# One operand of 16 blocks for the products of G and X in a chunked state recurrence

## The chip, the cores and the metric

The kernel runs on one core of one Trainium2 chip. The metric is the device time of one execution in microseconds, as the median of several executions; lower is better.

## The reference

The program is one attention-like recurrence followed by two feed-forward layers. Only the recurrence is touched by the change.

```python
B, H, S, D = 4, 8, 768, 40
for t in range(S):
    y[:, :, t] = einsum('bhd,bhde->bhe', r_t, state)
    Sa = einsum('bhde,bhe->bhd', state, a_t)
    state = state * w_t - einsum('bhd,bhe->bhde', Sa, b_t) + einsum('bhd,bhe->bhde', v_t, k_t)
x = y.transpose(0, 2, 1, 3).reshape(B * S, H * D)          # 3072 tokens of 320
x = moe(x)    # 8 experts of 1024, each token to its best one
x = moe2(x)   # 320 -> 2048 -> 320 with h * sigmoid(1.702 h)
```

## The kernel before

**Chunks.** The 768 steps are cut into 24 chunks of 32 steps. The 4 batches of 32 steps fill the 128 partitions, the 8 heads lie along the free axis. Inside a chunk the steps depend on one another through products of pairs of steps, so that a chunk needs four masked 32x32 matrices for each head and batch: G (k with a), X (v with r), Z (U with r) and the inverse T of a triangular matrix H (b with a). Every value is kept as a pair of fp16 numbers, high and low, and a product is the sum of three fp16 matmuls.

**From pair product to operand.** `pairs` makes the 32x32 products of one kind, 32 small matmuls for 8 heads, in the one PSUM bank "g". `masked` takes them out of the bank: a scalar_tensor_tensor on VectorE multiplies by the triangular mask into an fp32 tile `mx`, a copy to fp16 makes the high half, a subtraction the low half (`mgG`, `mgX`, `mgZ`). `bd` then spreads the four batches onto the diagonal of a 128x128 block for each head, by four operations, each a multiplication with a column of zeros and ones (`own`) that writes one stripe of 32 columns of all blocks. Each of the four may go to VectorE or ScalarE. The operands are `Gbd`, `Xbd`, `Zbd` and `Tbd`, [128, 2, 8, 128] fp16 each, one buffer each.

**Order of a chunk c.** `place(c)` spreads G and T (and fills `Nbd` and `KB`), `prep(c + 1)` loads k, v, r of the next chunk, splits and transposes them by DMA and makes the next G and X. `chain(c, g)` runs for two groups of four heads: W = Gbd v + (a with the state), then U by T, N and T again, then the state's update. `state` splits the new state for chunk c + 1. `output(c)` spreads X and Z and sums, in the PSUM bank "y", Xbd k + (r with the old state) + Zbd b; the sum is copied out to `Y` by VectorE. The state passes from chunk to chunk; the output doesn't feed the next chunk.

**What sets the order.** All instructions of the recurrence, the routing of tokens and the start of the first feed-forward layer go into a planner (`Plan`), which records reads and writes, and emits every engine's instructions in one fixed order. It works with a table of costs and with priorities by the longest path, and it chooses the engine wherever an operation is given as `either`. An engine then takes its instructions strictly in that order. Almost all rows of this stage show the line 234, where the planner issues. Names are therefore the key: `w<-vst,gbd` is the G product that opens a chunk's chain, `y<-kst,xbd` the X product of its output, `g<-rE,UE` its Z pairs, `y<-bst,zbd` (or `y<-xg,zbd`) its Z product, `S<-s,P` the new state. The copies of k stand in three buffers (`kst0` to `kst2`, chunk number modulo 3), those of v in two.

After the recurrence come the first feed-forward layer (lines 856 to 889) and the second (lines 1122 to 1165).

Of the kernel before, what the change touches and what calls it, by code (L numbers as in the profile page):

```python
# [9 lines left out]
F32 = mybir.dt.float32  # L10
# [456 lines left out]
F32 = mybir.dt.float32  # L467
F32R = mybir.dt.float32r
F16 = mybir.dt.float16
# [791 lines left out]
RING = 3  # L1261
PX, MX, MGX, SSB, V16B, UEB, SDB, PN = 4, 2, 2, 1, 2, 1, 2, 3
AHEAD = 1500
# [13 lines left out]
class Attn:  # L1277
# [7 lines left out]
    def __init__(self, tc, ctx, W, AB, KVR, keep, lent):  # L1285
# [6 lines left out]
        cp = self.cp = ctx.enter_context(tc.tile_pool(name="ac", bufs=1))  # L1292
# [13 lines left out]

        o64 = cp.tile([128, 64], F32, name="o64")
        nc.vector.memset(o64, 1.0)
        self.sel = cp.tile([128, 64], F32, name="sel")
        s2 = cp.tile([128, 64], F32, name="s2")  # L1310
        for dst, base in ((self.sel, 0), (s2, -32)):
# [44 lines left out]
        zero = lambda n, sh: self._zero(n, sh)  # L1356
        self.Gbd, self.Tbd, self.Nbd = (zero(n, [128, 2, 8, 128]) for n in ("gbd", "tbd", "nbd"))
        on = self.on
# [10 lines left out]
        for b2 in range(2):  # L1369
            for j in range(3):  # L1370
                r = slice(64 * b2, 64 * b2 + 64)
                nc.gpsimd.affine_select(self.pick[r, b2, j % 2, 40 * j:40 * j + 40], on[r, 0:40], pattern=[[1, 40]],
                                        compare_op=ALU.is_equal, fill=0.0, base=0, channel_multiplier=-1)
        self.Xbd, self.Zbd = (zero(n, [128, 2, 8, 128]) for n in ("xbd", "zbd"))

# [74 lines left out]
    def early(self, q):  # L1450
        nc = self.nc
        M = self.M[q // 2]
        u = slice(16 * (q % 2), 16 * (q % 2) + 16)
        BA = self.big()[:, 0:1280].rearrange("p (k h e) -> p k h e", k=2, e=40)
        nc.sync.dma_start(out=BA.rearrange("p k h e -> p k (h e)"), in_=self.AB[q])

        B, A = self.Bst[q % RING], self.Ast if q != 1 else self.Bst[RING - 1]
        for k, (st, f, lo, dup) in enumerate(((B, M["F"], 40, 80), (A, M["R"], 80, 40))):
            x = BA[:, k]
            nc.either(("vector", "tensor_tensor", (x, x, f[:, u, :]), dict(op=ALU.mult)))  # L1460
            self.twice(st, x, dup)
            nc.either(("vector", "tensor_tensor", (st[:, :, lo:lo + 40], x, st[:, :, 0:40]), dict(op=ALU.subtract)))
        bE = self.p1.tile([128, 16, 128], F16, tag="bE", name="bE") if q != 1 else \
            self.HU.bitcast(F16).rearrange("p t s -> p (t s)").rearrange("p (h x) -> p h x", h=16)
        aE = self.cp.tile([128, 16, 128], F16, name=f"aE{q}") if q < RING else self.E[q - RING]
        self.E[q] = aE
        nc.sync.dma_start_transpose(out=bE, in_=B.rearrange("p h x -> p (h x)"))
        nc.sync.dma_start_transpose(out=aE, in_=A.rearrange("p h x -> p (h x)"))
        H = self.pairs(bE, aE, 16)
        nc.scalar.activation(self.H[:, u, :], H, AF.Copy, scale=1.0 / (SK * SA))  # L1470
        N = self.pn.tile([128, 2, 16, 16], F16, tag="N")
        nc.scalar.activation(N[:, 0], H[:, :, 16:32], AF.Copy, scale=2.0 ** -6)
        nc.vector.scalar_tensor_tensor(N[:, 1], H[:, :, 16:32], 2.0 ** -6, N[:, 0], op0=ALU.mult, op1=ALU.subtract)
        self.N[q] = N

    def pairs(self, L, R, n):

        ps = self.pg.bank([n, 32], "g")
        for i in range(n):
            for b in range(4):  # L1480
                s = slice(32 * b, 32 * b + 32)
                self.nc.tensor.matmul(ps[s, i, :], lhsT=L[0:120, i, s], rhs=R[0:120, i, s], start=True, stop=True)
        return ps
# [67 lines left out]
    def masked(self, ps, scale, tag):  # L1551
        nc = self.nc
        n = ps.shape[1]
        x = self.p1.tile([128, n, 32], F32, tag="mx", name="mx", bufs=MX)
        nc.vector.scalar_tensor_tensor(x, ps, scale, self.mask.rearrange("p (o t) -> p o t", o=1).to_broadcast([128, n, 32]),
                                       op0=ALU.mult, op1=ALU.mult)
        g = self.p2.tile([128, 2, n, 32], F16, tag="mg" + tag, name="mg", bufs=MGX if tag == "X" else 2)
        nc.either(("scalar", "copy", (g[:, 0], x), {}), ("vector", "tensor_copy", (g[:, 0], x), {}))
# [3 lines left out]
    def prep(self, c):  # L1562
# [22 lines left out]
        C["rE"], C["k"], C["v"] = E[2], k, v  # L1585
        C["G"] = self.masked(self.pairs(E[0], aE, 8), 2.0 ** -6, "G")
        C["X"] = self.masked(self.pairs(E[1], E[2], 8), 2.0 ** -6, "X")

    def place(self, c):
# [3 lines left out]
        allh = slice(0, 8)  # L1593
        self.bd(self.Gbd, C["G"], allh)
        self.bd(self.Tbd, M["T"][c % 4], allh)
# [27 lines left out]
    def chain(self, c, g):  # L1623
# [6 lines left out]
        W = self.pw.bank([4, 64], f"w{g}")  # L1630
        self.mm3([(W[:, i, :], bd(self.Gbd, 4 * g + i), hl(C["v"], 4 * g + i)) for i in range(4)], True, c == 0)
        if c:
# [71 lines left out]
    def output(self, c, Sd, Y):  # L1704
# [5 lines left out]
        allh = slice(0, 8)  # L1710
        self.bd(self.Xbd, C["X"], allh)
        self.bd(self.Zbd, self.masked(self.pairs(C["UE"], C["rE"], 8), 2.0 ** -6, "Z"), allh)
        Yp = self.py.bank([8, 64], "y")
        self.mm3([(Yp[:, h, :], bd(self.Xbd, h), hl(C["k"], h)) for h in range(8)], True, False)
        if c:
# [210 lines left out]
```

## Time and profile before

| what | us |
|---|---|
| median of three runs (1107.86 to 1114.8) | 1113.67 |
| the profiled execution, its own time | 1103.53 |
| its span in the trace | 1101.8 |
| recurrence: from the start to the last copy of Y | 0 to 552 |
| end of the recurrence and start of the first layer | 552 to 600 |
| first layer | 600 to 760 |
| second layer | 760 to 1101.8 |

The profiled execution is a fourth run, a little faster than the three. The trace gives each instruction's start and end on its engine: PE is TensorE, DVE VectorE, ACT ScalarE. The four stretches follow each other, so that a microsecond taken out of the first moves everything behind it forward.

### The profile page before, as it was taken

How to read it: one execution, taken by the hardware profiler on the slowest of the kernel's cores; microseconds unless marked ns; L12 is line 12 of the kernel's file. 1: busy time of each engine (PE TensorE's matmuls, PEld its weight loads, DVE VectorE, ACT ScalarE, POOL GpSimd, SP SyncE). 2: the span in 40 equal slices, each digit the busy share in tenths (PEclk: the TensorE clock that was granted, in tenths of full speed). 3: DMA queues.
4: the chain of work that ended last, by engine and by line, in shares of the span. 5: the costliest groups of instructions: out<-in, count | busy, mean ns of one | idle time of the engine just before them, and what ended most of it. 6: DMA issues, size and time to landing. Idle time of an engine off the chain costs nothing. (4 is left out here: it accounts for less than half of the span.)

```text
span 1101.8 us, 37172 instructions
## 1 busy us (share of the span) xinstructions
PE 904.4 (82%) x15647; PEld 666.7 (61%) x15647; DVE 859.0 (78%) x2083; ACT 686.3 (62%) x1490; POOL 141.3 (13%) x225
## 2 busy tenths in 40 slices
PE   0167886876888887887569998998999999999995
PEld 0155665665667665666458877885555555555553
DVE  8998998999999999997565687777666666666652
ACT  4477998898899899886513364444443434343432
POOL 2000000020020030013031223212011111111101
PEclk9998897888666668788789999999999999999998
DMA  3669779689979789879525456445011111111100
GB/s 114 126 146 181 142 162 174 117 169 190 181 154 187 134 155 176 133 130 134 106 85 189 119 203 233 133 121 171 7 30 43 36 38 36 41 37 38 37 1 24
DMA packets 236014, 127.61 MB, mean 116 GB/s; under 512 B 219632, under 2 KB 222960, under 8 KB 234544
## 3 DMA queue, kind: packets, MB, share of 16 engines
q1 hardware_dynamic: 229680, 94.49, 46.5%
q0 software_dynamic: 6144, 30.54, 8.9%
q8 instruction: 125, 2.05, 0.8%
q14 instruction: 65, 0.53, 0.2%
HBM read 59.09 MB, written 12.16 MB: 65 GB/s over the span
## 5 line engine op out<-in xcount | busy, mean ns | idle before, releaser
L1138 ACT ACTIVATE sg<-t 128x512 f32<-128x512 f32 x96 | 60.5, 630 | 185.8 <-DVE t L1136 185.8
L1132 PE MATMUL h<-xT,WH 128*128 128x512 f16 x480 | 119.3, 379 | 3.0 <-DMA YS<-ys 2.3
L1156 PE MATMUL acc<-OH,gh 128*128 128x320 f16 x384 | 114.8, 299 | 0.5 <-ACT gh L1144 0.5
L1156 PE MATMUL acc<-OH,gl 128*128 128x320 f16 x384 | 114.8, 299 | 0.3 <-DVE gl L1148 0.3
L1156 PE MATMUL acc<-OL,gh 128*128 128x320 f16 x384 | 114.8, 299 | 0.0
L1136 DVE TENSOR_TENSOR t<-h,sB 128x512 f32<-128x512 f32 x96 | 66.2, 689 | 49.9 <-PE h L1132 49.9
L1156 PEld LDWEIGHTS <-gh 128*128 128x128 f16 x768 | 75.1, 98 | 43.6 <-ACT gh L1144 0.8
L1148 DVE TENSOR_TENSOR gl<-g,gh 128x512 f16<-128x512 f32 x96 | 66.3, 691 | 45.0 <-ACT gh L1144 45.0
L871 PE MATMUL h<-xT,split 128*128 128x128 f16 x1536 | 92.6, 221 | 5.4 <-DVE hl L874 2.3
L871 PEld LDWEIGHTS <-split 128*128 128x128 f16 x1536 | 89.7, 99 | 9.0 <-issue 4.1
L234 POOL DMA_INDIRECT XD<-XR,desti x24 | 31.2, 1302 | 468.5 <-ACT TT L234 206.9
L884 PE MATMUL y<-split,hh 128*128 128x320 f16 x384 | 82.3, 299 | 3.1 <-ACT split L846 1.3
L1132 PE MATMUL h<-xT,WL 128*128 128x512 f16 x288 | 77.8, 379 | 0.0
L1132 PEld LDWEIGHTS <-WH 128*128 128x128 f16 x480 | 46.5, 98 | 46.3 <-issue 2.6
L234 PE MATMUL w<-s,pick 128*128 128x160 f16 x368 | 62.8, 287 | 11.3 <-ACT s L234 4.1
L234 PEld LDWEIGHTS <-kb 64*128 64x128 f16 x2208 | 46.5, 101 | 33.0 <-issue 23.1
L234 PEld LDWEIGHTS <-tbd 128*128 128x128 f16 x1152 | 52.3, 106 | 21.9 <-issue 9.8
L1142 DVE SCALAR_TENSOR_TENSOR g<-h,sg 128x512 f32<-128x512 f32 x96 | 65.3, 680 | 0.0
L1144 ACT CAST gh<-g 128x512 f16<-128x512 f32 x96 | 59.2, 617 | 1.4 <-DVE g L1142 1.4
L1164 POOL DMA_INDIRECT out<-o,ti x24 | 23.4, 975 | 268.5 <-ACT o L1162 265.1
L884 PE MATMUL y<-split,hl 128*128 128x320 f16 x192 | 57.4, 299 | 0.0
L873 ACT ACTIVATE hh<-h 128x512 f16<-128x512 f32 x48 | 28.5, 594 | 38.8 <-PE h L871 38.5
(346 smaller groups left out, 2399.1 us busy)
## 6 DMA issues: line engine op xcount, KB each, us to landing
K<-in_KVR SPq DMA_DIRECT2D x24, 480.0 KB, 4.7
raw<-in_AB SPq DMA_DIRECT2D x13, 640.0 KB, 5.2
s<-in_wi SPq DMA_DIRECT2D x12, 512.0 KB, 4.6
s<-in_wo SPq DMA_DIRECT2D x10, 512.0 KB, 4.5
raw<-in_WU SPq DMA_DIRECT2D x6, 660.0 KB, 3.9
YS<-ys SPq DMA_DIRECT2D x24, 160.5 KB, 2.6
Sd<-s SPq DMA_TRANSPOSE x46, 4.4
raw<-in_KVR SPq DMA_DIRECT2D x1, 480.0 KB
```

Of the source, the lines that this page charges most:

```text
L234: r = self.made[i] = getattr(getattr(self.nc, e), op)(*a, **k)
L871: nc.tensor.matmul(h[:, f4, :], lhsT=a, rhs=b, start=(j == 0), stop=(j == 7))
L873: nc.scalar.activation(hh[:, s, :], h, AF.Relu)
L884: nc.tensor.matmul(y, lhsT=a[:, f, :], rhs=V(b, f), start=(n == 0), stop=(n == 23))
L1132: nc.tensor.matmul(h3, lhsT=a, rhs=r, start=(j == 0), stop=(j == 7))
L1136: nc.vector.tensor_tensor(t, hs[k], self.xs[steps[k][0]]["sB"], op=ALU.mult)
L1138: nc.scalar.activation(sgs[k], t, AF.Sigmoid, scale=1.702)
L1142: nc.vector.scalar_tensor_tensor(gs[k], hs.pop(k), 2.0 ** -4, sgs.pop(k), op0=ALU.mult, op1=ALU.mult)
L1144: nc.scalar.copy(ghs[k], gs[k])
L1148: nc.vector.tensor_tensor(gls[k], gs.pop(k), ghs[k], op=ALU.subtract)
L1156: nc.tensor.matmul(accs[c], lhsT=a[:, s], rhs=r[:, f, :], start=(f == 0 and j == 0), stop=(f == NF - 1 and j == 2))
L1164: sent.append(nc.gpsimd.indirect_dma_start(out=out, out_offset=bass.IndirectOffsetOnAxis(ap=X["ti"][:, c:c + 1], axis=0), in_=o, in_offset ...
```

## The change

G and X of a chunk are made together. `pairs` takes a list of operand pairs and writes 16 heads' worth of products into the whole bank "g". `masked` runs once over 512 columns instead of twice over 256, and `bd` spreads the 16 blocks into one operand `GXbd` [128, 2, 16, 128] with four operations of 1024 columns instead of eight of 512. That happens where G alone was spread before, in `place(c)`; `output(c)` reads blocks 8 to 15 of the same operand. The fp32 tile of `masked` now has a buffer for GX and one for Z (512 and 256 columns) in place of two that all three kinds shared (256 columns). A constant of the set-up borrows a piece of a large buffer. Z, T, N and KB are as before.

```diff
-PX, MX, MGX, SSB, V16B, UEB, SDB, PN = 4, 2, 2, 1, 2, 1, 2, 3
+PX, MX, MGX, SSB, V16B, UEB, SDB, PN = 4, 1, 2, 1, 2, 1, 2, 3
...
-        o64 = cp.tile([128, 64], F32, name="o64")
+        o64, s2 = self.bigs[0][:, 0:64], self.bigs[0][:, 64:128]
...
-        self.Gbd, self.Tbd, self.Nbd = (zero(n, [128, 2, 8, 128]) for n in ("gbd", "tbd", "nbd"))
+        self.GXbd = zero("gxbd", [128, 2, 16, 128])
+        self.Tbd, self.Nbd = (zero(n, [128, 2, 8, 128]) for n in ("tbd", "nbd"))
...
-    def pairs(self, L, R, n):
+    def pairs(self, what):
-        ps = self.pg.bank([n, 32], "g")
-        for i in range(n):
+        what = [(L[0:120, i], R[0:120, i]) for L, R, n in what for i in range(n)]
+        ps = self.pg.bank([len(what), 32], "g")
+        for i, (l, r) in enumerate(what):
             for b in range(4):
                 s = slice(32 * b, 32 * b + 32)
-                self.nc.tensor.matmul(ps[s, i, :], lhsT=L[0:120, i, s], rhs=R[0:120, i, s], start=True, stop=True)
+                self.nc.tensor.matmul(ps[s, i, :], lhsT=l[:, s], rhs=r[:, s], start=True, stop=True)
...
-        x = self.p1.tile([128, n, 32], F32, tag="mx", name="mx", bufs=MX)
+        x = self.p1.tile([128, n, 32], F32, tag="mx" + tag, name="mx", bufs=MX)
...
-        C["G"] = self.masked(self.pairs(E[0], aE, 8), 2.0 ** -6, "G")
-        C["X"] = self.masked(self.pairs(E[1], E[2], 8), 2.0 ** -6, "X")
+        C["GX"] = self.masked(self.pairs([(E[0], aE, 8), (E[1], E[2], 8)]), 2.0 ** -6, "G")
...
-        self.bd(self.Gbd, C["G"], allh)
+        self.bd(self.GXbd, C["GX"], slice(0, 16))
...
-        self.mm3([(W[:, i, :], bd(self.Gbd, 4 * g + i), hl(C["v"], 4 * g + i)) for i in range(4)], True, c == 0)
+        self.mm3([(W[:, i, :], bd(self.GXbd, 4 * g + i), hl(C["v"], 4 * g + i)) for i in range(4)], True, c == 0)
...
-        self.bd(self.Xbd, C["X"], allh)
-        self.bd(self.Zbd, self.masked(self.pairs(C["UE"], C["rE"], 8), 2.0 ** -6, "Z"), allh)
+        self.bd(self.Zbd, self.masked(self.pairs([(C["UE"], C["rE"], 8)]), 2.0 ** -6, "Z"), allh)
...
-        self.mm3([(Yp[:, h, :], bd(self.Xbd, h), hl(C["k"], h)) for h in range(8)], True, False)
+        self.mm3([(Yp[:, h, :], bd(self.GXbd, 8 + h), hl(C["k"], h)) for h in range(8)], True, False)
```

**What the planner makes of it.** The number of instructions on VectorE falls from 2713 rows to 2608, on ScalarE from 1691 to 1625; TensorE has the same 33233. Of the spreading operations of G and X, 86 were on VectorE and 106 on ScalarE; of the 96 of GX, 58 are on VectorE and 38 on ScalarE. Other work changes engine with it: VectorE gets 3 more spreading operations of T and Z together and 3 more splits of U, and gives 7 of `kb`, 2 other copies of k, v, r and the state, and 5 of the 1280-column copies of a and b to ScalarE. Of the copies to fp16 in `masked`, 23 of 72 were on VectorE, and now 18 of 48 (7 of them wide).

VectorE before, in the middle of the recurrence, where G of chunk 13 is spread (`mgG_1`). The copy `Y_0<-y` is that of chunk 10's output:

```order
L234 TENSOR_SCALAR s160_209<-S320_217 128x8x2x40
L234 SCALAR_TENSOR_TENSOR TT_3_248<-split1_152,TT_3_248 128x256
L234 TENSOR_TENSOR s160_209<-S320_217,s160_209 128x8x40
L234 SCALAR_TENSOR_TENSOR XR_0_278<-Y_0_275,sc_0_281,XR_0_278 128x256
L234 SCALAR_TENSOR_TENSOR XR_0_278<-Y_0_275,sc_0_281,XR_0_278 128x64
L234 TENSOR_SCALAR kb_226<-kst1_203,par_211 128x16x40
L234 TENSOR_TENSOR S321_218<-s_0_265,P_1_242 128x320
L234 TENSOR_SCALAR gbd_219<-mgG_1_258,own_212 128x16x32
L234 SCALAR_TENSOR_TENSOR Y_0_275<-y_0_234,split2_153 128x320
L234 TENSOR_SCALAR s161_210<-S321_218 128x8x2x40
L234 TENSOR_TENSOR K_0_249<-K_0_249,F_173 128x320
```

It stands behind the spreading of chunk 13's G. The same engine after the change, where GX of chunk 12 is spread (`mgG_0`; `Y_0<-y` is again chunk 10's output):

```order
L234 SCALAR_TENSOR_TENSOR mxG_0_250<-g_0_235,mask_214 128x512
L234 TENSOR_TENSOR s160_207<-S320_215,s160_207 128x8x40
L234 SCALAR_TENSOR_TENSOR XR_0_273<-Y_0_269,sc_0_276,XR_0_273 128x256
L234 TENSOR_REDUCE split1_152<-raw2_151 128x8x8
L234 SCALAR_TENSOR_TENSOR XR_0_273<-Y_0_269,sc_0_276,XR_0_273 128x64
L234 TENSOR_REDUCE split1_152<-raw1_150 128x8x8
L234 SCALAR_TENSOR_TENSOR Y_0_269<-y_0_231,split2_153 128x320
L234 TENSOR_TENSOR mgG_0_251<-mxG_0_250,mgG_0_251 128x512
L234 TENSOR_TENSOR S321_216<-s_0_259,P_1_239 128x320
L234 STREAM_TRANSPOSE split1_152<-split1_152 128x32x32
L234 TENSOR_SCALAR s161_208<-S321_216 128x8x2x40
L234 TENSOR_SCALAR gxbd_217<-mgG_0_251,own_210 128x32x32
```

The copy of the output moved from behind chunk 13's operand to ahead of chunk 12's.

TensorE before, at the start of chunk 13's chain (`w0<-vst1`); `y<-kst2,xbd` is the X product of chunk 11:

```order
L234 MATMUL y_0_234<-kst2_204,xbd_228 128x54
L234 LDWEIGHTS xbd_228
L234 MATMUL y_0_234<-kst2_204,xbd_228 128x54
L234 LDWEIGHTS gbd_219
L234 MATMUL w0_0_260<-vst1_206,gbd_219 128x54
```

The X product of chunk 11 stands among the first products of chunk 13. After the change, the end of the same X product (the rows behind it, `y<-Sd0,rE`, are the next part of the same output):

```order
L234 MATMUL y_0_231<-kst2_202,gxbd_217 128x54
L234 LDWEIGHTS gxbd_217
L234 MATMUL y_0_231<-kst2_202,gxbd_217 128x54
L234 LDWEIGHTS rE_2_278
L234 MATMUL y_0_231<-Sd0_0_266,rE_2_278 32x40
```

and, 188 rows on, the start of chunk 12's chain (`w0<-vst0`):

```order
L234 MATMUL s_0_259<-vst0_203,kb_224 128x54
L234 LDWEIGHTS kb_224
L234 MATMUL s_0_259<-vst0_203,kb_224 128x54
L234 LDWEIGHTS gxbd_217
L234 MATMUL w0_0_254<-vst0_203,gxbd_217 128x54
```

The X product of a chunk now ends ahead of the next chunk's W in all 23 places, by 90 to 460 rows; before, it ended 102 to 1056 rows behind it. A chunk has some 960 rows on this engine.

## Rows read from the trace of the kernel before

**Rows 1.** The page, busy tenths in 40 slices of the span.

```profile
DVE  8998998999999999997565687777666666666652
ACT  4477998898899899886513364444443434343432
```

**Rows 2.** Busy time of each engine in stretches of the recurrence.

```profile
core 0: us, PE busy (x) PEld busy (x) DVE busy (x) ACT busy (x) POOL busy (x), PEclk, DMA share, GB/s
75.00:500.00 425.00, 342.84 (x9977) 278.39 (x9976) 396.16 (x1102) 382.56 (x909) 28.12 (x32) 0.78 0.92 158
500.00:552.00 52.00, 31.84 (x938) 27.33 (x933) 34.70 (x138) 29.79 (x75) 9.82 (x18) 0.79 0.74 119
```

**Rows 3.** Groups by line and shape, 0 to 560 us: busy us, mean ns, idle before.

```profile
L234 DVE SCALAR_TENSOR_TENSOR mx<-g,mask 128x256 f32<-128x256 f32 x72 | 29.8, 415 | 10.2 <-PE g L234 9.7 <-PE w L234 0.3
L234 DVE TENSOR_TENSOR mgG<-mx,mgG 128x256 f16<-128x256 f32 x24 | 10.0, 415 | 0.0
L234 ACT CAST mgG<-mx 128x256 f16<-128x256 f32 x15 | 6.2, 410 | 6.2 <-DVE mx L234 6.2
L234 DVE TENSOR_SCALAR gbd<-mgG,own 128x512 f16<-128x512 f16 x55 | 17.7, 348 | 0.0
L234 DVE TENSOR_SCALAR nbd<-N,upper 128x256 f16<-128x256 f16 x96 | 23.9, 277 | 0.0
L234 ACT ACTIVATE gbd<-mgG,own 128x512 f16<-128x512 f16 x41 | 28.5, 724 | 3.4 <-DVE mgG L234 3.4
L234 ACT ACTIVATE xbd<-mgX,own 128x512 f16<-128x512 f16 x65 | 47.8, 748 | 0.3 <-PE y L234 0.3
L234 ACT ACTIVATE kb<-kst,par 128x640 f16<-128x640 f16 x32 | 26.5, 837 | 0.6 <-DVE kst L234 0.6
L234 PE MATMUL w<-vst,gbd 128*128 128x54 f16 x576 | 29.7, 205 | 11.5 <-ACT gbd L234 7.0 <-ACT Ss L234 3.1 <-ACT kst L234 1.3
```

**Rows 4.** The page's costliest groups: forms of twice the width, in the second layer.

```profile
L1142 DVE SCALAR_TENSOR_TENSOR g<-h,sg 128x512 f32<-128x512 f32 x96 | 65.3, 680 | 0.0
L1144 ACT CAST gh<-g 128x512 f16<-128x512 f32 x96 | 59.2, 617 | 1.4 <-DVE g L1142 1.4
L1148 DVE TENSOR_TENSOR gl<-g,gh 128x512 f16<-128x512 f32 x96 | 66.3, 691 | 45.0 <-ACT gh L1144 45.0
```

**Rows 5.** VectorE's timeline: start us, length us, then the instruction.

```profile
248.36 0.61 DVE L234 TENSOR_SCALAR gbd<-mgG,own 128x512 f16<-128x512 f16 x2
252.98 0.86 DVE L234 TENSOR_SCALAR nbd<-N,upper 128x256 f16<-128x256 f16 x4
...
305.42 0.42 DVE L234 SCALAR_TENSOR_TENSOR mx<-g,mask 128x256 f32<-128x256 f32 x1 [0.34 <-PE w L234]
305.76 0.48 DVE L234 TENSOR_SCALAR ust<-w 128x320 f16<-128x320 f32 x1
...
1000.05 0.69 DVE L1136 TENSOR_TENSOR t<-h,sB 128x512 f32<-128x512 f32 x1 [0.69 <-PE h L1132]
1000.65 0.68 DVE L1142 SCALAR_TENSOR_TENSOR g<-h,sg 128x512 f32<-128x512 f32 x1
```

**Rows 6.** ScalarE's timeline, the same columns.

```profile
209.65 1.94 ACT L234 ACTIVATE gbd<-mgG,own 128x512 f16<-128x512 f16 x3
259.18 1.58 ACT L234 ACTIVATE kb<-bst,par 128x640 f16<-128x640 f16 x2
```

**Rows 7.** Tiles gbd, xbd, Y: ns shortest/median/longest, first and last start us.

```profile
L234 PE MATMUL w<-vst,gbd x576: 185/199/253, 56.3 to 516.8; 128*128 128x54 f16 x192
L234 PE MATMUL y<-kst,xbd x576: 185/186/253, 87.7 to 541.4; 128*128 128x54 f16 x192
L234 DVE SCALAR_TENSOR_TENSOR Y<-y,R x12: 474/482/492, 173.8 to 551.8; 128x320 f32<-128x320 f32 x12
```

**Rows 8.** TensorE's timeline at chunk 9's output.

```profile
254.37 0.41 PE L234 MATMUL g<-rE,UE 120*32 120x32 f16 x32
259.48 0.74 PE L234 MATMUL y<-bst,zbd 128*128 128x54 f16 x23
```

More of the change, by code (lines that the diff above doesn't have):

```diff
@@ L1305, in __init__ @@
         self.clear(self.one.rearrange("p a b -> p (a b)"))
-        o64 = cp.tile([128, 64], F32, name="o64")
+        o64, s2 = self.bigs[0][:, 0:64], self.bigs[0][:, 64:128]
         nc.vector.memset(o64, 1.0)
         self.sel = cp.tile([128, 64], F32, name="sel")
-        s2 = cp.tile([128, 64], F32, name="s2")
         for dst, base in ((self.sel, 0), (s2, -32)):
@@ L1373, in __init__ @@
                                         compare_op=ALU.is_equal, fill=0.0, base=0, channel_multiplier=-1)
-        self.Xbd, self.Zbd = (zero(n, [128, 2, 8, 128]) for n in ("xbd", "zbd"))
+        self.Zbd = zero("zbd", [128, 2, 8, 128])
         self.viol = keep.tile([128, 12], F32, name="viol")
@@ L1468, in early @@
         nc.sync.dma_start_transpose(out=aE, in_=A.rearrange("p h x -> p (h x)"))
-        H = self.pairs(bE, aE, 16)
+        H = self.pairs([(bE, aE, 16)])
         nc.scalar.activation(self.H[:, u, :], H, AF.Copy, scale=1.0 / (SK * SA))
@@ L1553, in masked @@
         n = ps.shape[1]
-        x = self.p1.tile([128, n, 32], F32, tag="mx", name="mx", bufs=MX)
+        x = self.p1.tile([128, n, 32], F32, tag="mx" + tag, name="mx", bufs=MX)
         nc.vector.scalar_tensor_tensor(x, ps, scale, self.mask.rearrange("p (o t) -> p o t", o=1).to_broadcast([128, n, 32]),
                                        op0=ALU.mult, op1=ALU.mult)
-        g = self.p2.tile([128, 2, n, 32], F16, tag="mg" + tag, name="mg", bufs=MGX if tag == "X" else 2)
+        g = self.p2.tile([128, 2, n, 32], F16, tag="mg" + tag, name="mg", bufs=MGX)
         nc.either(("scalar", "copy", (g[:, 0], x), {}), ("vector", "tensor_copy", (g[:, 0], x), {}))
```

## The prediction

> **What bounds the kernel now.** The change touches only the recurrence, 0 to 552 us, so I first ask what is full there. The page's forty slices [rows 1] show VectorE at eight or nine tenths from the start to slice 20 and ScalarE close to it from slice 5 on; both fall off behind the recurrence. The table by stretches makes that a number [rows 2]: from 75 to 500 us VectorE is busy for 396.16 of 425 us (93%), ScalarE for 382.56 (90%), the DMA engines have a mean share of 0.92 and TensorE, at a granted clock of 0.78 of full speed, is busy for 81%. No single chain sets the pace here: chunks follow each other every 20.0 us (the W product's rows, tile gbd, first start 56.3, last 516.8, 23 chunks [rows 7]), and the idle time in front of all the W products is 11.5 us, of which 7.0 us waited for the operand gbd [rows 3]. So the pace is set by the instructions of VectorE and ScalarE, with VectorE the fuller by a little. In the last stretch, 500 to 552 us, VectorE is busy for only 34.70 of 52 us [rows 2]: that is the latency of the last outputs, the last copy of Y starting at 551.8, 35.0 us behind the last W product [rows 7].
>
> **How an operation is to be priced.** An instruction's duration isn't what it takes from its engine. Two spreads of 512 columns on VectorE last 0.61 us together [rows 5] while one lasts 0.348 [rows 3]: the second starts 0.26 us behind the first. Four of 256 columns last 0.86 us, one 0.277: 0.19 us each. So 256 columns more cost 0.066 us, and one of 1024 should hold VectorE for 0.26 + 2 x 0.066 = 0.39 us, against 2 x 0.26 = 0.52 for the pair that it replaces. On ScalarE three of 512 columns last 1.94 us [rows 6], one 0.724 [rows 3], so 0.61 each; two of 640 last 1.58 us, one 0.837, so 0.74. By the durations 128 columns add 0.113 us, by the spacing 0.13; one of 1024 thus holds ScalarE for 1.06 to 1.14 us, and I take 1.1, against 1.22 for the pair. The masked reading of the bank: the operation behind a 256-column one starts 0.34 us later [rows 5], one of 512 columns in the second layer holds the engine for 0.60 us (1000.05 to 1000.65 [rows 5]), so a pair of 0.66 to 0.68 becomes 0.60. The same holds for the subtraction, which has the same 0.415 us at 256 columns [rows 3] and 0.691 at 512 [rows 4].
>
> **The sum, part by part.** *Spreading, VectorE:* 86 operations x 0.26 = 22.4 us before, 58 x 0.39 = 22.6 after: +0.2 us, since the planner now gives VectorE 60% of them instead of 45%. *Spreading, ScalarE:* 106 x 0.61 = 64.7 us, after 38 x 1.1 = 41.8: -22.9 us. *Mask and subtraction, VectorE only:* 24 chunks x 2 x (0.66 - 0.60) = -2.9 us. *Copies to fp16:* ScalarE's 49 narrow ones (0.410 us long [rows 3], some 0.31 apart as an estimate from the 0.1 by which its other operations overlap) become 17 wide (0.617 [rows 4], so 0.51) and 13 narrow: 15.2 to 12.7, -2.5 us; VectorE's are about even. *Work that changes engine:* priced by width from the same rows, VectorE's 3 more T and Z spreads and 3 more U splits (+2.0), 7 fewer kb (-2.0), 2 fewer copies of 640 (-0.8) and 5 fewer of 1280 columns (-3.7) make -4.5 us; the mirror image puts about 9 us onto ScalarE. *Matmuls:* the same ones, 576 W and 576 X; no term. *Set-up:* the two zeroed operands become one of the same size, and the constants that move are below 1.5 us on either engine, beside a load that VectorE waits for; nothing. **VectorE: 0.2 - 2.9 - 4.5 = -7.2 us. ScalarE: -22.9 - 2.5 + 9 = -16.4 us.**
>
> If VectorE stays the fuller engine, the recurrence shortens by its 7.2 us: 1103.5 - 7.2 = 1096.3 us against the profiled execution. That execution lies 10 us below the median, so on the median's scale 1113.67 x 1096.3 / 1103.53 = 1106.4; I say 1106. The bounds of this term: by spacing with the planner's exchange left out, 2.7 us; by half of what both engines save together, 11.8 us.
>
> By whole durations, as if each instruction began only when the one ahead had ended, VectorE saves more: spreads 86 x 0.348 - 58 x 0.49 = 1.5, masks 24 x (0.83 - 0.68) = 3.6, subtractions 24 x (0.83 - 0.69) = 3.3, and some 5 of the exchange, 13.4 us in all, which gives 1090.1 and 1100 on the median's scale. The row of four spreads in 0.86 us, 0.25 us less than four times one [rows 3, 5], speaks against it. The Trainium skill, "VectorE: DVE Perf Modes", section "The DRAIN you can't avoid", says that the next operation doesn't start until the pipeline has emptied, and adds that one that is not held starts earlier; by the first half the sum would be this larger one, by this case's rows it is the smaller.
>
> **What the change adds: a wait.** With one buffer for both operands, chunk c + 1's GX can be written only when chunk c's X product has read its half. Before, the two had nothing to do with each other: the X product's rows (tile xbd) start 31.4 us behind the W product's in the first chunk and 24.6 us in the last [rows 7], which is more than a period, so X of chunk c came behind W of c + 1 everywhere. Now X of c must end, four writes must follow, and only then may W of c + 1 start. X of c in turn waits until Y of c - 1 has left the bank "y", and that for Z of c - 1. So the output, which nobody waited for, becomes part of a loop over two chunks: W, U, transposed U, Z, Y, X, GX, W. Behind a W that waits on TensorE stand the whole chain of its chunk and the state, and behind the waiting spreads on ScalarE and VectorE whatever the planner put there. Can the loop hold 2 x 20 us? From the Z pairs to the last Z product chunk 9 needed 5.85 us (254.37 to 259.48 + 0.74 [rows 8]); add Y (0.48 [rows 7]), 24 X products of some 0.03 us each (23 Z products took 0.74 [rows 8]), four writes on two engines (2 x 0.39 and 2 x 1.1 side by side, 2.2 us): 9.3 us and a few hand-overs from Z's pairs to the next W, out of a period of 20. There is room, unless Z's pairs come late. So I take the wait as 0 in the forecast; its upper bound is the four writes in full, some 2 us in each of 23 chunks, 46 us. Also, G's mask now waits for the last of three transposes (r) where it needed only k; the planner has placed that earlier, and the price is in the same bound.
>
> **The rivals.**
> *More comes back than VectorE's part.* ScalarE is lightened by 16 us and hands the chain's small copies over sooner, so that VectorE, which waits for some of them, loses part of its 29 idle us; and since outputs can't lag, fewer of them remain in the last 52 us, of which 17 are idle on VectorE [rows 2]. With half of both engines' saving (11.8) and 5 us of that tail, 16.8 us: 1086.7, on the median's scale 1097. For it: the planner balances the two engines. Against: static order, and DMA at 0.92. The reading by durations ends in the same region (1100).
> *The loop binds: slower.* The place is the spreading of GX, between X of c and W of c + 1, which the order shows 90 to 260 rows (2 to 5 us) apart in all but one chunk. The price is the part of the four writes and of the longer mask, copy and subtraction (0.75 us more in a row by [rows 3, 4]) that W waits for: 1 us in each of 23 chunks makes 23 - 7.2 = +16, so 1119 and 1130 on the median's scale; 2 us each, 1153. It decides once Y of c - 1 leaves its bank less than about 3 us before the state for chunk c + 1 is ready. For it: W already waited 7.0 us for gbd [rows 3].
> *Something else sets the pace.* The DMA share of 0.92 [rows 2] holds the transposes of k, v, r, U and the state, which don't change; if their rate is the limit, nothing moves: 1113.
>
> **How the numbers follow.** Forecast 0.43, more comes back 0.29, nothing moves 0.11, the loop binds 0.17. The four runs before spread by 1%, so about 1% is what a measurement can tell from no change. The forecast lies 0.7% below, so it counts as the same with some of its width beyond 1%: faster 0.32 (the second case and a little of the first), same 0.51, slower 0.17. For 8 in 10 the range goes down to the fast rival's 1097 less the width of a few us in which the runs scatter, 1091, and up over no change into the cheap end of the loop, 1126.
>
> **What would show it.** Right: the 256-column masks of G and X gone, 24 of 512 columns at about 0.68 us; spreads of 1024 columns at about 0.49 us on VectorE and 1.15 to 1.2 on ScalarE; VectorE still above 90% busy in the middle and ScalarE clearly lower, near 87%; the last copy of Y some 7 us earlier; idle time in front of W products not above the 11.5 us of now. Wrong: idle time before W that waits for gxbd, of the order of a microsecond for each chunk, and idle spells of both engines between Y and the spreading; or a period of 20 us unchanged although both engines have become emptier.

## The result, and the profile after

The changed kernel takes 1122.89 us (six runs, 1121.37 to 1125.53), the kernel before 1113.54 in the same measurement (six runs, 1104.0 to 1114.8): a ratio of 1.0108, 95% interval 1.0083 to 1.0133. The forecast was 0.7% faster; it is 1.1% slower. The profiled execution of the changed kernel took 1125.17 us. That of before (1103.53) lies just under the fastest of its six runs, so the 21.6 us between the two profiles are more than the 9.4 us between the medians, and I use the profiles for where time lies and the runs for how much it is.

The page of the changed kernel, busy tenths in 40 slices, beside [rows 1]:

```profile
DVE  8997898799799799697655688677766666666652
ACT  4467797798699699686722456445344435343432
```

Busy time by stretches, columns as in [rows 2]:

```profile
75.00:500.00 425.00, 326.82 (x9437) 265.88 (x9437) 373.96 (x973) 352.61 (x798) 18.54 (x32) 0.76 0.87 152
500.00:552.00 52.00, 36.83 (x1105) 30.96 (x1104) 37.07 (x135) 33.65 (x81) 8.86 (x16) 0.82 0.78 161
```

VectorE was to stay above 90% from 75 to 500 us. It is at 373.96 of 425, 88%: not a fuller engine with less to do, but an emptier one. The groups by shape, 0 to 580 us, that answer to [rows 3, 4]:

```profile
L234 ACT ACTIVATE gxbd<-mgG,own 128x1024 f16<-128x1024 f16 x38 | 42.7, 1152 | 3.8 <-DVE mgG L234 3.6
L234 PE MATMUL w<-vst,gxbd 128*128 128x54 f16 x576 | 29.5, 206 | 16.8 <-ACT gxbd L234 11.8 <-ACT Ss L234 3.2 <-DVE bst L234 1.0
L234 DVE TENSOR_SCALAR gxbd<-mgG,own 128x1024 f16<-128x1024 f16 x58 | 26.3, 479 | 0.3 <-PE y L234 0.3
L234 DVE SCALAR_TENSOR_TENSOR mxG<-g,mask 128x512 f32<-128x512 f32 x24 | 16.4, 685 | 2.0 <-PE g L234 1.8
L234 DVE TENSOR_TENSOR mgG<-mxG,mgG 128x512 f16<-128x512 f32 x24 | 16.4, 684 | 0.9 <-ACT mgG L234 0.9
L234 ACT CAST mgG<-mxG 128x512 f16<-128x512 f32 x17 | 10.5, 616 | 3.0 <-DVE mxG L234 2.9
```

The sizes are those that were priced: 0.479 and 1.152 us for a spread, 0.685 for a mask. The W product now waits 16.8 us, of them 11.8 for gxbd (11.5 and 7.0 in [rows 3]). Most of the 11.8 stands in front of the very first W product, before any loop has begun. TensorE's rows there, before and after:

```profile
56.33 1.26 PE L234 MATMUL w<-vst,gbd 128*128 128x54 f16 x24 [2.08 <-ACT gbd L234]
62.62 1.26 PE L234 MATMUL w<-vst,gxbd 128*128 128x54 f16 x24 [8.41 <-ACT gxbd L234]
```

In the other 23 chunks W waits 3.4 us for gxbd, where it waited 4.9 for gbd. So the loss isn't a wait of W for its operand. The tiles, with first and last start, beside [rows 7]:

```profile
L234 PE MATMUL w<-vst,gxbd x576: 185/208/253, 62.6 to 550.6; 128*128 128x54 f16 x192
L234 DVE SCALAR_TENSOR_TENSOR Y<-y,R x12: 479/483/492, 170.8 to 569.1; 128x320 f32<-128x320 f32 x12
```

W starts 6.3 us later in the first chunk and 33.8 us later in the last; the last output follows 18.5 us behind the last W instead of 35.0. Cut at these three times (first W, last W, last Y), the recurrence reads as follows; the third busy figure is VectorE, the fourth ScalarE. Before:

```profile
0.00:56.30 56.30, 4.32 (x220) 3.47 (x220) 50.81 (x124) 27.33 (x38) 5.84 (x34) 1.00 0.51 117
56.30:516.80 460.50, 368.72 (x10673) 299.37 (x10674) 430.62 (x1217) 407.64 (x973) 36.82 (x47) 0.79 0.92 158
516.80:551.80 35.00, 17.02 (x463) 14.87 (x460) 18.52 (x65) 17.21 (x43) 0.93 (x4) 0.76 0.52 107
```

After:

```profile
0.00:62.60 62.60, 4.19 (x220) 3.45 (x220) 57.24 (x129) 28.69 (x39) 5.89 (x34) 1.00 0.54 129
62.60:550.60 488.00, 372.71 (x10754) 304.58 (x10754) 421.36 (x1131) 393.76 (x896) 27.40 (x48) 0.77 0.86 153
550.60:569.10 18.50, 14.67 (x376) 12.47 (x369) 14.90 (x50) 13.97 (x39) 0.00 (x0) 0.91 0.09 17
```

The end of such a stage is VectorE's busy time plus its idle time, and that sum splits the loss. Busy: 50.81 + 430.62 + 18.52 = 499.95 before, 57.24 + 421.36 + 14.90 = 493.50 after, 6.45 less. Idle between the first and the last W: 460.5 - 430.62 = 29.9 before, 488.0 - 421.36 = 66.6 after, 36.7 more. Idle in the tail: 16.5 before, 3.6 after, 12.9 less. Idle ahead of the first W is the same (5.5 and 5.4). Together -6.45 + 36.7 - 12.9 - 0.1 = +17.3 us, which is by how much the last Y moved (551.8 to 569.1). A further 4.3 us of the two spans' 21.6 lie behind it. Of these, 2.8 are the start of the first layer, 23.7 instead of 20.9 us after the last Y: a scatter of routed rows on GpSimd, behind which the last rows wait, began 0.3 us ahead of the last Y before (551.53) and begins 2.4 us behind it now (571.47).

### The profile page after: what moved, and what is told of

Read it like the earlier page. It is cut to its first block, busy times and chain, and to the rows that moved or that the text cites. A ratio compares the mean times of both kernels' runs of the same rounds, so it can differ in the third digit from the quotient of the medians.

```text
span 1123.4 us, 37005 instructions
## 1 busy us (share of the span) xinstructions
PE 909.1 (81%) x15647; PEld 671.1 (60%) x15647; DVE 853.1 (76%) x1993; ACT 672.0 (60%) x1411; POOL 131.7 (12%) x224
## 5 line engine op out<-in xcount | busy, mean ns | idle before, releaser
L234 POOL DMA_INDIRECT XD<-XR,desti x24 | 24.1, 1006 | 517.8 <-ACT V L234 278.9
L234 PE MATMUL w<-s,pick 128*128 128x160 f16 x368 | 59.0, 273 | 15.0 <-ACT Ss L234 6.2
L234 PEld LDWEIGHTS <-gxbd 128*128 128x128 f16 x1152 | 47.9, 107 | 23.6 <-ACT gxbd L234 14.4
```

Source lines behind the costliest of these rows:

```text
L234: r = self.made[i] = getattr(getattr(self.nc, e), op)(*a, **k)
```

## The experiments

Three theories. **Theory 1:** the tie (W of chunk c + 1 behind X of chunk c, behind Y and Z of c - 1, behind the transposed U) costs some 1%. **Theory 2:** the wide mask and its wait for r stand in the way of W. **Theory 3:** the planner's new order is worse by chance. Measurements fell on different chips and times, in which the kernel before took about 1095 or about 1112 us; each kernel is compared with the runs of before that stand beside it. The parts of the change and the old U (below) were measured only where before takes about 1095 us.

**Parts of the change alone.** *Mask alone:* G and X share bank, mask and split, and are spread apart as before.

```diff
-        self.bd(self.GXbd, C["GX"], slice(0, 16))
+        self.bd(self.Gbd, C["GX"][:, :, 0:8], allh)
...
+        self.bd(self.Xbd, C["GX"][:, :, 8:16], allh)
```

> G and X share one bank, one mask, one split, as in the change; the spreads are the old ones, four of 512 columns into gbd with place and four into xbd with output. Theory 1 (the shared operand ties W of chunk c + 1 to X of chunk c, which costs 1.3 us in each chunk): without the shared operand the tie is gone, period back to 19.9 us, last Y 35 to 38 us behind the last W, time 1108 to 1114. Theory 2 (G's mask waits for the transposed r, and the wide mask and split lie in the path to W): the cost stays, period above 21 us, 1120 to 1128. Theory 3 (another order of the planner, good or bad by chance): anything from 1103 to 1125, with no tie between X and W.

Measured 1096.89 us, ratio 1.0026 (0.9986 to 1.0065). W starts at 63.7 us as late as after the change, but the loss isn't there. The wide mask and its wait for r (theory 2) carry no 1% here. That alone doesn't settle theory 2, because the whole change costs only 0.3% in measurements of this kind (below); the last pair of kernels does.

*Full width without the tie:* an operand of 24 blocks, in which X has two places in turn. To make room, `mgG` has one buffer instead of two and some tiles of the set-up lie in borrowed memory.

```diff
+        self.GXbd = zero("gxbd", [128, 2, 24, 128])
...
-self.pairs([(E[0], aE, 8), (E[1], E[2], 8)])
+self.pairs([(E[1], E[2], 8), (E[0], aE, 8)][::-1 if c % 2 else 1])
...
-        self.bd(self.GXbd, C["GX"], slice(0, 16))
+        self.bd(self.GXbd, C["GX"], slice(8 * (c % 2), 8 * (c % 2) + 16))
```

> The change with an operand of 24 blocks: G always in blocks 8 to 15, X in 0 to 7 in even chunks and in 16 to 23 in odd ones, so that every write is still one of 1024 columns, but X of chunk c need only be read before the writes of chunk c + 2. To make room mgG has one buffer instead of two, and some small tiles of the set-up lie in lent memory. Theory 1 (tie): the tie is one period looser, the outputs may lag again, period at or below 19.9 us, and the saving of the width comes out: 1100 to 1110, faster than before. Theory 2 (long operations and the wait for r ahead of W): nothing changes, 1120 to 1126. Theory 3 (order by chance): 1103 to 1125 without a pattern.

1094.87 us, ratio 1.0013 (0.9974 to 1.0051). Without the tie there is no slowdown, as theory 1 says, with the same reservation; but the kernel isn't faster either, against what theory 1 expected of it.

*Tie with wide spreads, narrow masks:*

```diff
+        GX = C["GX"] = self.p2.tile([128, 2, 16, 32], F16, tag="mgG", name="mg", bufs=MGX)
+        self.masked(self.pairs([(E[0], aE, 8)]), 2.0 ** -6, "G", GX[:, :, 0:8])
+        self.masked(self.pairs([(E[1], E[2], 8)]), 2.0 ** -6, "G", GX[:, :, 8:16])
```

> One operand of 16 blocks with four writes of 1024 columns, as in the change, but G and X are made, masked and split apart (two of 256 columns each), into the two halves of one tile. Theory 1 (tie): tied as the change is, minus the small saving of the wide masks (2.9 us of VectorE): 1121 to 1128, period about 21.3 us, last Y under 25 us behind the last W. Theory 2 in the part that blames the wide mask and split: 1110 to 1116; in the part that blames the wait for r: 1120 to 1126 as theory 1. Theory 3: no pattern.

1102.75 us, ratio 1.0089 (1.0056 to 1.0122).

*The tie alone,* with the masks of the last one and eight spreads of 512 columns:

```diff
-        self.bd(self.GXbd, C["GX"], slice(0, 16))
+        for a in range(2):
+            self.bd(self.GXbd[:, a:a + 1], C["GX"][:, a:a + 1], slice(0, 16))
```

> The tie alone: one operand of 16 blocks, but masks and splits of 256 columns as before, and eight spreads of 512 columns, each over all 16 heads of the high or of the low half. As many operations of the same width as before, only that all eight stand between X of chunk c and W of chunk c + 1. Theory 1 (tie): slower than the change by what its width saved, 1126 to 1140, period above 21.4 us, last Y close behind the last W. Theory 2 (wide operations): near before, 1111 to 1117. Theory 3: no pattern.

1105.3 us, ratio 1.0111 (1.0076 to 1.0146). These four shared one chip: the two without the tie are at before's time, the two with it 0.9 and 1.1% above. The expected 1126 and more was reckoned from a measurement in which before took 1113; the ratio is what counts.

**The changed kernel again, and what sets the pace of before.** 

> The changed kernel once more, beside the others of this call on one chip, with a profile. Theory 1 (the tie costs about 1%): ratio 1.007 to 1.013, and last Y 15 to 22 us behind the last W. Theory 3 (chance of one measurement): ratio near 1.002, as in the two kernels without the tie.

1100.14 us, ratio 1.0035 (1.0001 to 1.007); last Y 21.0 us behind the last W. The tail is what theory 1 expected, the ratio is less (1.007 to 1.013 expected). A third measurement:

> The changed kernel a third time, to settle the size: it was 1.0108 against before on one chip and 1.0035 on another. If the price hangs on the chip's DMA latency, between 1.002 and 1.012 again, with the higher ratio where before is slower; last W to last Y 15 to 22 us.

1098.36 us, ratio 1.0027 (0.9991 to 1.0062). Where before takes 1095 us the change costs 0.3%, not 1%. The kernel before, unchanged, with a second profile:

> The kernel before with a profile on the same chip as the others of this call, so that its windows can be set beside theirs. All theories: within 1% of the other runs of the kernel before; period of a chunk about 2% under 19.9 us if the chip is the faster one of the first experiments.

1114.56 us in one run, while the other runs beside it had a median of 1095.38: single executions of the kernel before scatter by over 1%.

*Less VectorE work:* the low halves of X and Z are made only in the first two chunks.

```diff
+        if lo:
             nc.either(("vector", "tensor_tensor", (g[:, 1], x, g[:, 0]), dict(op=ALU.subtract)))
...
-        C["X"] = self.masked(self.pairs(E[1], E[2], 8), 2.0 ** -6, "X")
+        C["X"] = self.masked(self.pairs(E[1], E[2], 8), 2.0 ** -6, "X", c < 2)
```

> The kernel before without the subtractions that make the low halves of X and Z, from chunk 2 on (the old low halves are used): 44 VectorE operations of 0.415 us fewer, which hold the engine for 0.33 us each, 14.5 us. None of them feeds the next state. If VectorE's occupancy sets the pace, as the sum of the prediction assumed: 14 us shorter, ratio about 0.987. If something else does (DMA, or the chain from state to state): within 0.4% of before. A saving of 7 us of VectorE would then be worth nothing either.

1097.79 us, ratio 1.0035 (0.9996 to 1.0074): no gain from more VectorE work than the change saves. Its stretch from first to last W:

```profile
57.10:526.20 469.10, 366.78 (x10669) 298.14 (x10669) 421.25 (x1200) 400.12 (x951) 34.90 (x47) 0.80 0.93 160
```

Busy 9.4 us less than before's 430.62, idle 47.9 where it was 29.9: in this stretch, what is taken from the engine comes back as waiting. The tail is shorter, 18.3 us instead of 35.0, so that the last Y stands at 544.5 us against 551.8; but these two profiles come from different measurements, and by the runs nothing is gained.

*Fewer DMA transposes:* the state's transposes for the output stop after chunk 1.

```diff
+        if c < 2:
             nc.sync.dma_start_transpose(out=Sd.rearrange("p a h x -> p (a h) x"), in_=S16.rearrange("p a h x -> p (a h x)"))
```

> The kernel before without the transposes of the state for the output (Sd), from chunk 2 on (the old ones are used, so later outputs and with them the routing and the layers behind are other ones; what counts is the recurrence in the profile): 44 of some 200 DMA transposes fewer. If the DMA engines (0.92 busy) set the pace: the period falls by more than 1.5 us and the DMA share falls below 0.85 only a little, last Y 30 us or more earlier. If VectorE sets it: the period stays at before's, and only the DMA share falls.

1084.78 us, ratio 0.9912 (0.9881 to 0.9943), DMA share 0.75. The stretch between the W products is 453.5 us instead of 460.5, 0.3 us a chunk: less than the 1.5 that a DMA limit would have given, more than nothing. The later outputs are other ones and with them the routing, so the stretch counts here and not the ratio.

*A shorter chain:* the correction V no longer enters U.

```diff
-        times(Up, self.Tbd, V16, False, skip_group_check=True)
```

> The kernel before, with the last T product left out of the chain (T times V, the correction, so U is another one): V is still computed, masked and copied, but U and the state no longer wait for it. 24 matmuls a chunk fewer, the same instructions on VectorE and ScalarE. What counts is the recurrence in the profile. If the chain from state to state sets the pace: X to V to U takes 2.5 to 3 us of each group in the trace of before, so the period falls by 1.5 us or more, 35 us in all, ratio about 0.97. If an engine's occupancy (VectorE, ScalarE, DMA) sets it: period within 0.4 us of before's.

1099.75 us, ratio 1.0045 (1.0016 to 1.0075); W to W 458.9 us, at a mean granted clock of TensorE of 0.75 instead of 0.79, which may have taken back a part. The 1.5 us a chunk that a limit by the chain from state to state would have given aren't there. None of the three, taken alone, sets the pace.

**What the tie waits for.** Z from the transposed U of the chunk before, in two buffers, once in the changed kernel, once in the kernel before (the output is another one in both):

```diff
-self.pairs([(C["UE"], C["rE"], 8)])
+self.pairs([(self.C[max(c - 1, 0)]["UE"], C["rE"], 8)])
```

> The changed kernel, but Z is made from the transposed U of the chunk before (UE in two buffers; the output is another one, the number of instructions is the same). The tie between X of c and W of c + 1 stays, but what X waits for (Y of c - 1, hence Z of c - 1) no longer waits for a DMA transpose that was just issued. If the tie costs what it does because the transpose of U now lies in the loop of the state: the recurrence is back at or below before's, waits for UE near 0, ratio 0.995 to 1.002. If the tie costs by itself (engine order, long writes ahead of W): as the changed kernel, 1.004 to 1.011.

1086.13 us, ratio 0.9887 (0.9804 to 0.997, from four runs): faster than expected.

> The control to the run with the tie: the kernel before with Z made from the transposed U of the chunk before. There the transpose of U lies outside the loop, the output only lags: within 0.4% of before by every theory, unless the stream of DMA waits itself slows the state's chain, then up to 0.5% faster.

1096.49 us, ratio 0.9984 (0.9949 to 1.002). The two ran on one chip, beside the third measurement of the changed kernel (1.0027). With the tie and all of the width, but without the wait for U's transpose, the kernel is 1.1% faster than before, while the same edit gives the untied kernel 0.2%. The stretches first W to last W, last W to last Y, with the tie:

```profile
60.40:524.30 463.90, 378.59 (x10878) 309.35 (x10879) 431.33 (x1163) 395.23 (x913) 30.87 (x48) 0.78 0.92 161
524.30:527.70 3.40, 2.90 (x118) 2.45 (x114) 3.40 (x13) 3.40 (x11) 1.52 (x1) 1.00 0.00 0
```

and without:

```profile
61.80:538.60 476.80, 374.45 (x10922) 305.63 (x10923) 436.68 (x1259) 419.68 (x996) 37.76 (x48) 0.80 0.90 157
538.60:542.10 3.50, 3.50 (x96) 3.22 (x94) 2.74 (x9) 2.83 (x9) 1.61 (x3) 0.54 0.02 5
```

In both the tail is gone: the last Z needs no fresh U. With the tie VectorE's idle time between the W products is 32.6 us, without it 40.1: here the tie costs nothing.

**Other orders of the same work.** One number of the planner is changed, in the kernel before and in the changed one.

```diff
-HOLD = 0.2
+HOLD = 0.22
```

> The kernel before, with one number of the planner changed (it holds an engine for a more urgent operation up to 0.22 instead of 0.20 of an operation's cost): the same instructions in another order. If a plan's chance is worth 1% (theory 3): ratio anywhere between 0.99 and 1.01. If the planner's orders are about equally good and the differences come from the change's tie: 0.997 to 1.003.

1109.2 us, ratio 0.9972 (0.9941 to 1.0003).

> The changed kernel with the first of the two planner numbers changed (0.22). Theory 1 (tie with the transposed U in it): the price stays under another order, 1.003 to 1.011, waits for UE above 10 us, last Y 15 to 25 us behind the last W. Theory 3 (chance of one plan): ratio as scattered as for the kernel before and not on one side of it.

1129.17 us, ratio 1.0132 (1.0077 to 1.0188).

```diff
-BIAS = 0.7
+BIAS = 0.72
```

> As the run before, with the other number of the planner changed (the cost by which it compares two engines weighted 0.72 instead of 0.70): again the same work in another order, some operations on another engine. Theory 3: between 0.99 and 1.01. Else 0.997 to 1.003.

1107.64 us, ratio 0.9946 (0.9917 to 0.9974).

> The changed kernel with the second of the two planner numbers changed (0.72). Theory 1: 1.003 to 1.011 again. Theory 3: on either side of the kernel before, between 0.99 and 1.01.

1127.8 us, ratio 1.0122 (1.0062 to 1.0181). A plan's chance is worth up to 0.5% (the 0.4% of the kernels with less VectorE work and with the shorter chain lie within it), but the pairs don't overlap: three orders of the changed kernel lie 1.0 to 1.3% above, where before takes some 1112 us, two of them a little above what theory 1 expected. Theory 3 falls.

**The tie's price on one chip,** both kernels of full width:

> The untied kernel of full width (X in blocks 0 to 7 or 16 to 23 in turn) again, now on the same chip as the changed kernel, so that the two differ only in the tie (and in one buffer of mgG). Theory 1 (the tie with the transposed U in it is the price): ratio 0.995 to 1.003, and 0.3 to 1.2% below the changed kernel of the same call. Theory 3: no order between the two. That the width itself is worth nothing shows again if this one does not fall under 0.995.

1110.33 us, ratio 1.0003 (0.9978 to 1.0029).

> The changed kernel beside the untied one on the same chip. Theory 1: above it by 0.3 to 1.2%, by more where the kernel before takes 1112 us than where it takes 1095; ratio to before 1.003 to 1.012. Theory 3: within the interval of the untied one.

1124.07 us, ratio 1.0101 (1.0044 to 1.0158). In this measurement the tie costs 13.7 us, and without it the width is worth nothing. The untied kernel has the wide mask and the wait for r as well, so theory 2 falls. First to last W, last W to last Y, the untied kernel:

```profile
58.00:536.20 478.20, 368.73 (x10720) 302.46 (x10721) 423.36 (x1123) 393.01 (x906) 34.53 (x48) 0.80 0.88 158
536.20:553.30 17.10, 13.94 (x402) 11.36 (x399) 14.99 (x48) 14.38 (x39) 0.00 (x0) 1.00 0.24 51
```

and the changed one beside it:

```profile
62.60:547.60 485.00, 373.32 (x10754) 304.10 (x10754) 421.43 (x1131) 394.15 (x896) 27.87 (x48) 0.77 0.86 154
547.60:565.80 18.20, 14.41 (x377) 12.20 (x369) 14.89 (x50) 14.03 (x39) 0.00 (x0) 0.91 0.09 17
```

VectorE idles 54.8 us between the W products without the tie and 63.6 with it.

## Why the prediction was wrong, point by point

**The prices of the operations were right.** VectorE's busy time fell by 6.45 us (forecast 7.2), ScalarE's from 27.33 + 407.64 + 17.21 = 452.18 to 28.69 + 393.76 + 13.97 = 436.42, 15.8 us (forecast 16.4). The reading by whole durations would have had 13.4 us for VectorE. The changed kernel's own rows show the spacing too: four spreads of 1024 columns in 1.67 us, 0.479 for one, so 0.40 apart (0.39 priced).

```profile
262.63 1.67 DVE L234 TENSOR_SCALAR gxbd<-mgG,own 128x1024 f16<-128x1024 f16 x4
```

The Trainium skill, "VectorE: DVE Perf Modes", section "The DRAIN you can't avoid", says that the next operation starts only behind the emptied pipeline, and adds that one that is not held starts earlier. These rows go with the second half: a spread starts 0.40 us behind the last, which takes 0.479.

**The first step that failed: "If VectorE stays the fuller engine, the recurrence shortens by its 7.2 us".** VectorE at 93% was read as the pace. The untied kernel of full width has the saving and no shorter time (1.0013, 1.0003): between the W products VectorE idles 462.6 - 423.31 = 39.3 us in its first profile and 54.8 in its second, against 29.9 and 464.2 - 429.89 = 34.3 in the two of before. Taking 9.4 us of that stretch's work from VectorE in the kernel before gave 1.0035, with 18 us more idle time. These stretches leave out the tail; that nothing was gained is by the runs. VectorE's remaining 7% were waits for other engines and for DMAs, and taking work from VectorE brought no gain. Fewer DMA transposes, less VectorE work and a shorter state chain each moved the stretch between the W products by -7.0, +8.6 and -1.6 us, where a plan's chance is about 5 us. Which of them would have to shrink together stays open.

**The second, which made the sign: "I take the wait as 0 in the forecast".** The loop was seen and priced by its length (9.3 us out of a period of 20), as if only a loop longer than the period could cost. Where before takes some 1112 us, as in the measurement that the forecast was made for, the tie costs 13.7 us at full width (1.0003 against 1.0101 on one chip). Where before takes some 1095 us, the tie by itself costs 1.1% (1.0111), but at full width its price isn't clear of noise (1.0027 and 1.0035 with it, 1.0013 without). VectorE's idle time between the W products is much the same there: 35.6 and 42.0 us with the tie (third and second measurement), 39.3 without (*Full width without the tie*). The three in this order:

```profile
62.50:518.40 455.90, 360.91 (x10754) 295.76 (x10754) 420.33 (x1131) 393.53 (x896) 29.60 (x47) 0.82 0.91 158
62.60:525.00 462.40, 361.74 (x10753) 297.30 (x10753) 420.44 (x1131) 394.36 (x895) 29.62 (x47) 0.80 0.89 156
58.10:520.70 462.60, 365.83 (x10719) 299.49 (x10720) 423.31 (x1121) 390.76 (x904) 31.42 (x47) 0.81 0.90 158
```

So at full width the loop has room where nothing disturbs it, as the prediction said, and W hardly waits for gxbd in it. What the prediction left out is that the output's lag was slack. The reading that fits the two kernels of full width: a disturbance, at the scatters of the last section, is taken up by the lag of the untied kernel and goes into the state's chain of the tied one. It doesn't explain the 1.1% of the tie by itself, which was measured without such a disturbance; that stays open. That the transposed U lies in the loop counts as well: with an old U the tied kernel goes from 1.0027 to 0.9887, the untied one only to 0.9984. But the old U wasn't measured where the tie costs 13.7 us, so how much of that price passes through U, Z and Y stays open. The idle time of TensorE for UE alone doesn't decide it: from 75 to 520 us, on the weight load's side, in the kernel before, in the changed one, and in the untied one of full width (last experiment):

```profile
PEld L234 <- DMA UE<-ust: 5.7, 3, 2.5
```

```profile
PEld L234 <- DMA UE<-ust: 14.9, 9, 4.4
```

```profile
PEld L234 <- DMA UE<-ust: 13.2, 9, 3.1
```

The columns are us in all, times and longest. The last kernel waits nearly as long for UE as the changed one, without the loss.

**The rivals.** "The loop binds: slower" (0.17) had the sign and the tie right, but not the place or the price, so its number is in part luck. It put 1 us in each chunk on W's wait for the spreading of GX, 23 us less the saving, 16 in all; the medians moved by 9.4, and W waits for gxbd no longer in the loop than before (3.4 and 4.9 us). "It decides once Y of c - 1 leaves its bank less than about 3 us before the state" looks too strict by the reading above, but no run measures it. "More comes back" had the shorter tail right (idle there 12.9 us less), but a part of the routing came behind the last Y (2.8 us). Its gain by a lighter ScalarE didn't come.

**Where the width may be worth something.** The tie alone is at 1.0111, with wide spreads at 1.0089, with wide masks as well at 1.0035 and 1.0027 (the last two on other chips, before at 1095 us in all). That is 0.8% in all, the size of the forecast, as if the width repaid a part of the tie's price. But the spreads' 0.2% lies within the intervals, and the masks' 0.6% compares different chips and is hardly more than a plan's chance; why they should count only under the tie isn't shown.

**The baseline.** The profile of before shows an execution 10 us under its median. None of the waits of the last section is in it; a single profile was not the kernel's usual run.

## What to carry to other kernels

Two operands with different readers, laid into one buffer so that one instruction may write both, share one lifetime: look at which reader is the later one, and whether its lag was the slack that kept the other's loop full; if so, give the late half two places in turn (1.0003 instead of 1.0101 in one measurement here). A busy share of 93% doesn't make an engine the pace: write the stage's end as its busy plus its idle time, and ask of a saving which wait ends earlier by it. Where a planner orders the work anew, its chance (here up to 0.5%) has to be measured with a change that does nothing, before 1% is explained.

## What the runs showed of the hardware that I hadn't expected

In the measurements in which the kernel before takes some 1112 us, TensorE falters while GpSimd scatters the routed rows. In the changed kernel of the last experiment, TensorE and GpSimd at 294 us:

```profile
294.82 0.48 PE L234 MATMUL w<-W,tbd 128*128 128x54 f16 x2
295.85 0.25 PE L234 MATMUL w<-W,tbd 128*128 128x54 f16 x3 [0.55 <-issue]
296.62 0.33 PE L234 MATMUL w<-W,tbd 128*128 128x54 f16 x4 [0.53 <-issue]
297.37 0.30 PE L234 MATMUL w<-W,tbd 128*128 128x54 f16 x3 [0.41 <-issue]
```

```profile
293.84 0.98 POOL L234 DMA_INDIRECT XD<-XR,desti  x1 [75.48 <-DVE split L234]
295.12 0.96 POOL L234 DMA_INDIRECT XD<-XR,desti  x1 [0.19 <-issue]
296.39 0.96 POOL L234 DMA_INDIRECT XD<-XR,desti  x1 [0.19 <-issue]
297.65 0.96 POOL L234 DMA_INDIRECT XD<-XR,desti  x1 [0.19 <-issue]
```

The same twelve matmuls beside the same scatter, in the third measurement of the same program:

```profile
289.27 0.67 PE L234 MATMUL w<-W,tbd 128*128 128x54 f16 x12
```

They take 2.85 us (294.82 to 297.67) instead of 0.67, with pauses in which TensorE waits for nothing that the profile shows ("issue"). ScalarE and VectorE behind it then wait for something that the profile can't name ("remote"), in the same execution, 62 to 566 us:

```profile
ACT V L234 <- remote: 11.7, 2, 7.3
ACT ust L234 <- remote: 5.3, 2, 4.1
DVE ust L234 <- remote: 4.9, 1, 4.9
ACT X L234 <- remote: 4.7, 2, 2.6
DVE nbd L234 <- remote: 3.7, 1, 3.7
DVE S L234 <- remote: 3.0, 1, 3.0
```

33.3 us in all, some of them at the same time on both engines, at the scatters that follow each group of four chunks. Such waits stand in seven of the eight profiles from measurements with the slower before (9.4 to 33.3 us; the eighth is the first profile of before, which was faster than all runs beside it) and in none of the twelve others. TensorE's pauses of 0.25 us and more at the scatters go with them: 6 to 22 in each of the seven, at most 2 in the others.

What they cost can be read from the starts of W in the same program. The chunk ahead of the last scatters and the one behind them, in the last experiment and then in the third measurement:

```profile
521.30 0.48 PE L234 MATMUL w<-vst,gxbd 128*128 128x54 f16 x12 [0.45 <-DVE L L234]
546.70 0.74 PE L234 MATMUL w<-vst,gxbd 128*128 128x54 f16 x23 [0.70 <-ACT Ss L234]
```

```profile
501.95 0.47 PE L234 MATMUL w<-vst,gxbd 128*128 128x54 f16 x12 [0.42 <-DVE L L234]
517.51 0.74 PE L234 MATMUL w<-vst,gxbd 128*128 128x54 f16 x23 [0.78 <-ACT Ss L234]
```

25.4 us instead of 15.6. At the five scatters W slips by 3.5, 4.8, 4.9, 4.9 and 9.8 us, together 27.9 of the 29.2 us by which the last chunk's W starts later. The two kernels come out of it differently: the changed one's last Y moved from 539.4 to 565.8 (26.4 us), that of the untied one from 543.3 to 553.3 (10.0 us). The untied one's profile also has fewer of the pauses (8 against 20), so it may be hit less and not only bear it better. The difference is of the size that separates the change's 0.3% in one kind of measurement from its 1% in the other. No run leaves the scatters out or moves them, so that this is the cause fits the traces but isn't shown by an experiment. Nor are they all that makes an execution slow: the second profile of before, at 1114.56 us, has none of these waits. Why TensorE falters there in some measurements and not in others stays open.
